# V loads on a second queue, shorter load cycles and a shorter lead of the scores in a two-problem attention kernel

## The chip, the cores and the metric

The kernel runs on one core of a Trainium2 chip. A core has a matrix engine (TensorE, PE in the profile; its weight loads are the row PEld), VectorE (DVE), ScalarE (ACT), GpSimd (POOL) and SyncE (SP), which here only issues transfers. Each engine takes its instructions in the order of the program; between engines there are semaphores. Transfers between the main memory and the core's SBUF go over 16 DMA engines; a transfer is issued by an instruction on some engine's queue.

The metric is the device time of one execution in microseconds (us). The time before is the median of three runs, 1215.2 us (1215.15 to 1217.5). The profiled execution took 1209.51 us, with a span of 1207.8 us from its first to its last instruction.

## The reference

Two independent problems, A and B, of the same shape: 16 batches, 16 heads, 144 queries, 512 keys, a head size of 256, a model width of 448. Everything is bf16.

```python
q = (x @ wq).reshape(B, Sq, H, Dh).transpose(0, 2, 1, 3)
scores = jnp.einsum("bhqd,bhkd->bhqk", q, k_cache) * (Dh ** -0.5)
p = softmax(scores, axis=-1)
o = jnp.einsum("bhqk,bhkd->bhqd", p, v_cache)
y = o.transpose(0, 2, 1, 3).reshape(B, Sq, H * Dh) @ wo
```

The output is A's y beside B's y, (16, 144, 896).

## The kernel before, in words

**Units.** A unit U is one head of one batch: 256 units of A, then 256 of B, 512 in all (`NT`). Four units make a group G, whose V (1 MB) is one transfer; eight make a super-group SG, whose K (2 MB) is one transposing transfer. There are 64 super-groups (`NSG`).

**One unit.** Its 144 queries are split into 112 (part "a") and a remainder of 32 (part "b"). On PE, a unit has `Q` (8 matmuls, the projection; line 340), `SA` (2 matmuls, scores of part a; line 476), `TA` (4 transposes of the normalised probabilities; line 530), `PV` (8 matmuls; line 563) and a share of `OP`, the output projection (line 601), which is cut into pieces and fed in by a credit. The remainders of a super-group's eight units are packed by fours on the 128 partitions, and their scores `SB` (16 matmuls; line 380) come once for each super-group. Between scores and transposes, DVE takes the row maximum (line 488; 393 for the remainder), ACT the exponential with its sum (499; 403), DVE the reciprocal (509; 413), and GpSimd multiplies by it (517, `nm`; 421, `nmb`).

**The remainder's transpose.** It has two ways. Either PE transposes it (`t_tb`, line 443: 8 matmuls for each super-group, evacuated by DVE, line 453), or a transposing transfer SBUF to SBUF does it (`t_ptb_dma`, line 431, on SP's queue, which waits for `nmb`). The set `TB_SG` names the super-groups that go over PE: the first 8, and 28 to 37 around the step from A to B; 18 in all. Either way GpSimd then copies the result (`cptb`, line 463, twice for each super-group) to where `PV` reads it.

**Order.** A planner writes each engine's program slot by slot: slot i holds `PV(i)`, `TA(i + 2)`, and the scores of a unit further ahead. `LAGS` says how many units the scores of super-group n are ahead of its PV: 7, 5, 6, 7 and so on to 14 for n = 10 and later (`sb_slot[n] = 8n - lag`). `Q` is 8 units ahead of the scores.

**Transfers.** All are issued on SP's queue, in the order of a plan that is sorted by slot (`dma_plan`): x (lines 297, 298), wq (276, 278), wo (286), K (307), V (318), the remainder's transpose (431), stores (630). K has two buffers (`NK`), V five (`NV`), x two. From super-group 8 on the plan has a cycle of 16 units (t = 8n, n even): transpose of remainder n at t-4, K of n+2 at t-3, transpose of n+1 and K of n+3 at t+2, then three V at t+5 and one at t+8. So a K is issued 5 or 8 units before its SB. The wq of B are planned for slots 228.9 to 235, the wo of B for 277 and 293.

Of the kernel before, what the change touches and what calls it, by code (L numbers as in the profile page):

```python
# [12 lines left out]
PE, ACT, DVE, POOL, SP = "pe", "act", "dve", "pool", "sp"  # L13
# [109 lines left out]
def bass_concat_heads__mha_block_cached__gqa_block_cached__near_ridge_kernel(  # L123
# [15 lines left out]
    vs = (A_v_cache, B_v_cache)  # L139
# [20 lines left out]
    NPC = NWO // OPP  # L160

    LT = 2
    LAGS = (7, 5, 6, 7, 8, 9, 10, 11, 12, 13, 14)
    RAMP = 8
    TB_SG = set(range(RAMP)) | set(range(NSG // 2 - 4, NSG // 2 + 6))
    NK, NV, NXG = 2, 5, 2
    WO_AT = ((12, 18, 26, 33), (277, 277, 293, 293))
    OP_FROM = (34, 34)
    N_WARM = (12, 16)
    XB = 2  # L170
    assert Bn % XB == 0
    NQT, NPA, NPB, NPT, NST, NSTB, NOST = 12, 14, 2, 8, 4, 2, 3
    NPBT = 1
    RS = 4
    KR = 4
# [3 lines left out]
    NXGT = NP * Bn // XB  # L179
# [3 lines left out]
    with contextlib.ExitStack() as es:  # L183
        def sb(name, shape, dt):
            return es.enter_context(nc.sbuf_tensor(name, shape, dt))
# [12 lines left out]
        pb_sb = sb("pb_sb", [128, NPB, 2, SK], BF16)  # L198
        pt_sb = sb("pt_sb", [128, NPT, 4, SQ], BF16)
        pbt_sb = sb("pbt_sb", [128, NPBT, 2, 4, 128], BF16)  # L200
        ost_sb = sb("ost_sb", [128, NOST, D], BF16)
        ident = sb("ident", [128, 128], BF16)
        stat = sb("stat", [128, 3 * NST + 3 * NSTB + 2], F32)
# [108 lines left out]
        def t_load_v(G):  # L312
            pr, b, h0 = unit(4 * G)
            sl = G % NV
            src = vs[pr][b, h0:h0 + 4].rearrange("u (p c) d -> p u (c d)", p=128)

            def e(q):
                return q.dma_start(v_sb[:, sl, :, :], src).then_inc(sems["v%d" % sl], 16)
# [107 lines left out]
        def t_ptb_dma(SG):  # L426
            psl = SG % NPB
            tsl = SG % NPBT

            def e(q):  # L430
                return q.dma_start_transpose(pbt_sb[:, tsl, :, :, :].rearrange("p g c q -> p (g c) q"),
                                             pb_sb[:, psl, :, :].rearrange("p g k -> p (g k)")).then_inc(
                    sems["pb%d" % tsl], 16)
            S.add(SP, e, reads=[(("pb", psl, g), (2 * SG + g, 1)) for g in range(2)],
                  writes=[(("pbt", tsl, g), SG) for g in range(2)], dma_sem="pb%d" % tsl, name="pb%d" % SG)

        def t_tb(G):
            psl = (G // 2) % NPB
# [44 lines left out]
        def t_max(U):  # L483
# [3 lines left out]
            def e(v):  # L487
# [2 lines left out]
            S.add(DVE, e, reads=[(("sap", bank), ("s", U))], writes=[(("neg", sl), U)], banks=["sa%d" % bank],  # L490
                  name="mx%d" % U)

        def t_exp(U):
            bank = U % 2
            sl = U % NST
            psl = U % NPA

            def e(a):
                return a.activation(pa_sb[0:QA, psl, :], sa_ps[bank][0:QA, :], AF.Exp,  # L499
                                    bias=stat[0:QA, NEG + sl:NEG + sl + 1], scale=1.0,  # L500
                                    accum_out=stat[0:QA, RSUM + sl:RSUM + sl + 1])
            S.add(ACT, e, reads=[(("sap", bank), ("s", U)), (("neg", sl), U)],
                  writes=[(("pa", psl), (U, 0)), (("rsum", sl), U)], banks=["sa%d" % bank], name="ex%d" % U)

        def t_recip(U):
            sl = U % NST
# [4 lines left out]

        def t_norm(U):
            sl = U % NST
            psl = U % NPA

            def e(g):
                return g.tensor_tensor(pa_sb[0:QA, psl, :], pa_sb[0:QA, psl, :],  # L517
                                       stat[0:QA, RINV + sl:RINV + sl + 1].to_broadcast([QA, SK]), op=ALU.mult)
            S.add(POOL, e, reads=[(("pa", psl), (U, 0)), (("rinv", sl), U)], writes=[(("pa", psl), (U, 1))],
                  name="nm%d" % U)  # L520

        def t_ta(U):
            psl = U % NPA
            bank = ta_bank[U]

            def e(t):
                src = pa_sb[0:QA, psl, :].rearrange("q (c p) -> q c p", c=4)
                ins = None
                for c in range(4):
                    ins = t.transpose(pta_ps[bank][:, c * 128:c * 128 + QA], src[:, c, :], ident[0:QA, 0:QA])  # L530
# [126 lines left out]
        def plan(at, lo, dl, fn, *args):  # L657
            assert lo <= at <= dl, (fn.__name__, args, lo, at, dl)
            dma_plan.append((at, len(dma_plan), fn, args))

        def plan_x(at, XG):
            n = XB * H
            plan(at, q_slot[(XG - 1) * n - 1] + 1 if XG >= NXG else s_min, q_slot[XG * n], t_load_x, XG)

        def plan_k(at, SG):
            plan(at, sa_slot[8 * (SG - NK) + 7] + 1 if SG >= NK else s_min, sb_slot[SG], t_load_k, SG)

        def plan_v(at, G):
            lo = 4 * (G - NV) + 3 + 1 if G >= NV else s_min
            plan(max(at, lo), lo, 4 * G, t_load_v, G)  # L670

        def plan_pb(at, SG):
            if SG not in TB_SG:
                plan(at, sb_slot[SG] + 5, 8 * SG - 1, t_ptb_dma, SG)

        plan_x(s_min, 0)
        for hg in range(HG):
            plan(s_min + (0 if hg < 2 else 1), s_min, q_slot[4 * hg], t_load_wq, 0, hg)
            if hg == 1:
                plan_k(s_min, 0)  # L680
        plan_v(s_min + 2, 0)
        for n in range(1, RAMP + 2):
            at = max(sb_slot[n] - 6, sa_slot[8 * (n - NK) + 7] + 1) if n >= NK else s_min + 2
            if n == 3:
                plan_x(at, 1)
            if n == 6:
                plan_x(at, 2)
# [58 lines left out]
        while True:  # L746
# [151 lines left out]
```

## Time and profile before

| What | Before |
|---|---|
| median of 3 runs | 1215.2 us |
| profiled execution, its own time | 1209.51 us |
| its span | 1207.8 us |
| PE busy | 1167.9 us (97%) |
| VectorE, ScalarE, GpSimd busy | 743.6, 747.8, 727.0 us |
| granted PE clock, mean | 0.994 of full |
| DMA | 306.18 MB, mean 254 GB/s |
| median time from issue to landing: K (A, B), V, remainder's transpose | 12.2 and 11.5, 9.0, 4.7 us |

Busy time of PE is modelled from pipelined matmuls, so a busy PE is not one at its peak. A DMA-issuing instruction does not count as busy time of its engine. A wait line reads: who waited, at which line, for whom; then the total in us, how often, and the longest. In a table by windows, the columns are the busy us of PE, PEld, DVE, ACT and POOL with the number of instructions, then the granted clock of PE, the DMA engines' busy share (over 1 where packets overlap) and GB/s. "SPq" is SP's queue: start, and how long the issuing instruction held the queue.

### The profile page before, as it was taken

The numbers are of one execution on the slowest core, as the hardware profiler recorded it, in microseconds if no ns is written. First come the engines' busy times: TensorE is split into PE (matmuls) and PEld (weight loads), VectorE is DVE, ScalarE is ACT, GpSimd is POOL, SyncE is SP. The second block draws the span as 40 slices with busy tenths as digits, with TensorE's granted clock in tenths as the row PEclk, the third lists the DMA queues.
The fourth block names the chain that finished last, engine by engine and source line by source line (L and its number), as shares of the span: only waits on it lengthen the run. The fifth ranks groups of instructions, "written<-read, shape, count | busy, mean of one in ns | idle before, by whom it ended". The sixth has DMA issues, their size and how long they took to land.

```text
span 1207.8 us, 33200 instructions
## 1 busy us (share of the span) xinstructions
PE 1167.9 (97%) x13612; PEld 875.3 (72%) x13612; DVE 743.6 (62%) x2088; ACT 747.8 (62%) x2213; POOL 727.0 (60%) x774
## 2 busy tenths in 40 slices
PE   6898999999999999999899999999999999999989
PEld 4676777777777777777577777777777777777766
DVE  3676666666666656666466665665666566566661
ACT  2565666666666666666466666666666666566662
POOL 1676576666666566666465665666666665666661
PEclk9999999999999999999899999999999999999999
DMA  9999999999999999999999899999999999999981
GB/s 243 284 262 294 283 277 188 253 264 269 268 283 206 264 253 293 259 263 245 288 249 255 249 265 277 261 279 251 268 236 248 253 292 274 231 251 252 249 207 56
DMA packets 679577, 306.18 MB, mean 254 GB/s; under 512 B 597504, under 2 KB 610304, under 8 KB 679424
## 3 DMA queue, kind: packets, MB, share of 16 engines
q1 hardware_dynamic: 679424, 304.05, 104.1%
q8 instruction: 107, 1.75, 0.6%
q14 instruction: 46, 0.38, 0.1%
HBM read 148.90 MB, written 4.13 MB: 127 GB/s over the span
## 4 chain that ended last, share of the span: by engine, by line
PE 81%; DMA 11%; POOL 3%; DVE 3%; SPq 1%; issue 1%; ACT 0%; DVEq 0%
PE ot_ps L563 18%; PE qp_ps L340 17%; PE sa_ps L476 17%; PE op_ps L601 16%; PE sa_ps L530 7%; DMA kt_sb<-in_B_k_cache_dram 6%; PE sb_ps L380 5%; DMA kt_sb<-in_A_k_cache_dram 5%; POOL pa_sb L517 2%; DVE stat L488 1%; SPq L307 1%; POOL pb_sb L421 1%; PE qp_ps L601 1%; PE sb_ps L443 0%; DVE qt_sb L353 0%
## 5 line engine op out<-in xcount | busy, mean ns | idle before, releaser
L517 POOL TENSOR_TENSOR pa_sb<-pa_sb,stat 112x512 bf16<-112x512 bf16 x512 | 531.4, 1039 | 453.0 <-DVE stat L509 427.4
L499 ACT ACTIVATE pa_sb<-sa_ps,stat 112x512 bf16<-112x512 f32 x512 | 352.1, 688 | 400.5 <-DVE stat L488 398.2
L488 DVE TENSOR_REDUCE stat<-sa_ps 112x1 f32<-112x512 f32 x512 | 353.8, 691 | 329.6 <-PE sa_ps L476 324.8
L340 PEld LDWEIGHTS qp_ps<-xt_sb,wq_sb 128*128 128x128 bf16 x4048 | 283.4, 98 | 81.6 <-DMA wq_sb<-in_A_wq_dram 3.6
L340 PE MATMUL qp_ps<-xt_sb,wq_sb 128*128 128x144 bf16 x4048 | 336.7, 226 | 5.0 <-DMA wq_sb<-in_A_wq_dram 4.7
L563 PE MATMUL ot_ps<-pt_sb,v_sb 128*128 128x144 bf16 x4096 | 341.5, 226 | 0.0
L476 PE MATMUL sa_ps<-kt_sb,qt_sb 128*112 128x512 bf16 x1024 | 312.6, 387 | 6.7 <-DVE pt_sb L540 5.2
L601 PE MATMUL op_ps<-wo_sb,ring 128*128 128x448 bf16 x1120 | 275.3, 353 | 0.0
L563 PEld LDWEIGHTS ot_ps<-pt_sb,v_sb 128*128 128x128 bf16 x4096 | 268.9, 98 | 0.4
L530 PEld LDWEIGHTS sa_ps<-ident,pa_sb 112*128 112x128 bf16 x2048 | 143.8, 97 | 119.0 <-ACT pa_sb L499 38.0
L540 DVE COPY pt_sb<-sa_ps 128x448 bf16<-128x448 bf16 x512 | 191.0, 373 | 19.8 <-PE sa_ps L530 19.8
L578 ACT ACTIVATE ring<-ot_ps 128x288 bf16<-128x288 f32 (+8 forms) x512 | 190.6, 372 | 19.2 <-PE ot_ps L563 19.2
L530 PE MATMUL sa_ps<-ident,pa_sb 112*128 112x112 bf16 x2048 | 185.9, 212 | 5.7 <-ACT pa_sb L499 5.7
L353 DVE TENSOR_SCALAR qt_sb<-qp_ps 128x288 bf16<-128x288 f32 x252 | 115.1, 457 | 93.4 <-PE qp_ps L340 91.6
L421 POOL TENSOR_TENSOR pb_sb<-pb_sb,stat 128x512 bf16<-128x512 bf16 x128 | 133.0, 1039 | 0.0
L476 PEld LDWEIGHTS sa_ps<-kt_sb,qt_sb 128*112 128x112 bf16 x1024 | 96.4, 130 | 46.3 <-issue 27.6
L357 ACT ACTIVATE qt_sb<-qp_ps 128x288 bf16<-128x288 f32 x254 | 105.3, 415 | 32.0 <-PE qp_ps L340 30.6
L601 PEld LDWEIGHTS op_ps<-wo_sb,ring 128*128 128x128 bf16 x1120 | 96.1, 98 | 31.9 <-issue 0.2
L499 ACT ACTIVATION_READ_ACCUMULATOR pa_sb<-sa_ps,stat 112x1 f32 x512 | 99.1, 193 | 0.0
L403 ACT ACTIVATE pb_sb<-sb_ps,stat 128x512 bf16<-128x512 f32 x128 | 88.5, 691 | 0.8
L393 DVE TENSOR_REDUCE stat<-sb_ps 128x1 f32<-128x512 f32 x128 | 87.2, 681 | 0.0
L463 POOL COPY pt_sb<-pbt_sb 128x512 bf16<-128x512 bf16 x128 | 78.0, 610 | 10.9 <-PE ot_ps L563 10.9
(33 smaller groups left out, 345.1 us busy)
## 6 DMA issues: line engine op xcount, KB each, us to landing
v_sb<-in_A_v_cache_dram SPq DMA_DIRECT2D x64, 1024.0 KB, 9.0
v_sb<-in_B_v_cache_dram SPq DMA_DIRECT2D x64, 1024.0 KB, 9.0
out_dram<-ost_sb SPq DMA_DIRECT2D x36, 112.0 KB, 9.5
wo_sb<-in_A_wo_dram SPq DMA_DIRECT2D x8, 448.0 KB, 9.3
wo_sb<-in_B_wo_dram SPq DMA_DIRECT2D x8, 448.0 KB, 5.3
wq_sb<-in_A_wq_dram SPq DMA_DIRECT2D x4, 768.0 KB, 6.0
wq_sb<-in_B_wq_dram SPq DMA_DIRECT2D x4, 768.0 KB, 10.5
pbt_sb<-pb_sb SPq DMA_TRANSPOSE x46, 4.7
```

The source lines that it names most:

```text
L340: ins = t.matmul(acc[:, dc * SQ:(dc + 1) * SQ], lhsT=wq_sb[:, kc, c0:c0 + 128], rhs=xt_sb[:, xsl, kc, xo:xo + SQ], start=(kc == 0 and dc = ...
L353: return v.tensor_scalar(qt_sb[:, sl, :, :], src, 1.0 / 16.0, None, op0=ALU.mult)
L421: return g.tensor_tensor(pb_sb[:, psl, G % 2, :], pb_sb[:, psl, G % 2, :], stat[:, RINVB + sl:RINVB + sl + 1].to_broadcast([128, SK]), op= ...
L476: ins = t.matmul(sa_ps[bank][0:QA, :].rearrange("q (k r) -> q k r", k=KR), lhsT=qt_sb[:, U % NQT, dc, 0:QA], rhs=kt_of(U, dc), start=(dc = ...
L488: return v.tensor_reduce(stat[0:QA, NEG + sl:NEG + sl + 1], sa_ps[bank][0:QA, :], axis=AX.X, op=ALU.max, negate=True)
L499: return a.activation(pa_sb[0:QA, psl, :], sa_ps[bank][0:QA, :], AF.Exp, bias=stat[0:QA, NEG + sl:NEG + sl + 1], scale=1.0, accum_out=stat ...
L517: return g.tensor_tensor(pa_sb[0:QA, psl, :], pa_sb[0:QA, psl, :], stat[0:QA, RINV + sl:RINV + sl + 1].to_broadcast([QA, SK]), op=ALU.mult)
L530: ins = t.transpose(pta_ps[bank][:, c * 128:c * 128 + QA], src[:, c, :], ident[0:QA, 0:QA])
L540: return v.tensor_copy(pt_sb[:, sl, :, 0:QA], pta_ps[bank][:, 0:512].rearrange("p (c q) -> p c q", c=4)[:, :, 0:QA])
L563: ins = t.matmul(ot_ps[ob][:, dc * SQ:(dc + 1) * SQ], lhsT=v_sb[:, vsl, j, c * DH + dc * 128:c * DH + (dc + 1) * 128], rhs=pt_sb[:, sl, c, ...
L578: ins = a.activation(ring[:, 2 * h:2 * h + 2, c0:c0 + n1], src[:, :, 0:n1], AF.Copy)
L601: ins = t.matmul(acc[0:m, 0:D], lhsT=ring[:, c, col0:col0 + m], rhs=wo_sb[:, c, :], start=(c == first), stop=(c == last))
```

## The change

- Every V but V0 is issued on GpSimd's queue. V0 stays on SP's, with a semaphore of its own.
- The plan's cycle of 16 units goes. Each K is issued as soon as the scores that read its buffer before are through, 8 units before its SB. Each V from group 5 on is issued one unit after its buffer's last PV (slot 4(G-5)+5); V1 to V4 at slots -2, 1, 4 and 7.
- `LAGS` becomes 5, 5, 6, 7, 8, 9, 10: the lead ends at 10 units and is reached with super-group 6 (unit 48).
- `TB_SG` is the first 6 super-groups only; the other 58 remainders go over the transposing transfer, planned 5 units before their PV.
- x, wq of B and wo are planned for other slots. The buffers are fewer: q 12 to 9, probabilities 14 to 11, output staging 3 to 2.
- A way to send parts "a" over the transfer too (`ADMA`) is in the text but empty, and so without effect.

```diff
     LT = 2
-    LAGS = (7, 5, 6, 7, 8, 9, 10, 11, 12, 13, 14)
-    RAMP = 8
-    TB_SG = set(range(RAMP)) | set(range(NSG // 2 - 4, NSG // 2 + 6))
+    LAGS = (5, 5, 6, 7, 8, 9, 10)
+    RAMP = 6
+    TB_SG = set(range(RAMP))
+    ADMA = ()
+    NPX = 2 + len(ADMA)
     NK, NV, NXG = 2, 5, 2
-    WO_AT = ((12, 18, 26, 33), (277, 277, 293, 293))
+    WO_AT = ((12, 17, 20, 28), (277, 281, 285, 289))
...
-    NQT, NPA, NPB, NPT, NST, NSTB, NOST = 12, 14, 2, 8, 4, 2, 3
+    NQT, NPA, NPB, NPT, NST, NSTB, NOST = 9, 11, 2, 8, 4, 2, 2
...
+        sem_names.append("vs")
...
-                return q.dma_start(v_sb[:, sl, :, :], src).then_inc(sems["v%d" % sl], 16)
-            S.add(SP, e, writes=[(("v", sl), G)], dma_sem="v%d" % sl, name="v%d" % G)
+                return q.dma_start(v_sb[:, sl, :, :], src).then_inc(sems["vs" if G == 0 else "v%d" % sl], 16)
+            S.add(SP if G == 0 else POOL, e, writes=[(("v", sl), G)], dma_sem="vs" if G == 0 else "v%d" % sl, name="v%d" % G)
...
         def plan_k(at, SG):
-            plan(at, sa_slot[8 * (SG - NK) + 7] + 1 if SG >= NK else s_min, sb_slot[SG], t_load_k, SG)
+            lo = sa_slot[8 * (SG - NK) + 7] + 1 if SG >= NK else s_min
+            plan(max(at, lo), lo, sb_slot[SG], t_load_k, SG)
...
-        def plan_pb(at, SG):
+        def plan_pb(SG):
             if SG not in TB_SG:
-                plan(at, sb_slot[SG] + 5, 8 * SG - 1, t_ptb_dma, SG)
+                plan(sb_slot[SG] + 5, sb_slot[SG] + 5, 8 * SG - 2, t_ptb_dma, SG)
...
-        plan_v(s_min + 2, 0)
-        for n in range(1, RAMP + 2):
-            at = max(sb_slot[n] - 6, sa_slot[8 * (n - NK) + 7] + 1) if n >= NK else s_min + 2
...
-            plan_k(at, n)
-            plan_v(at + 1, 2 * n - 1)
-            plan_v(at + 1, 2 * n)
+        plan_v(s_min, 0)
+        plan_k(s_min, 1)
+        for G in range(1, NV):
+            plan_v(sb_slot[0] + 3 * G, G)
+        for XG in range(1, NXGT):
+            t = XB * H * XG
+            plan_x(t - (30 if XG < 2 else 33.5), XG)
+        for SG in range(NSG):
+            plan_pb(SG)
+            if SG >= NK:
+                plan_k(sa_slot[8 * (SG - NK) + 7] + 1, SG)
+        for G in range(NV, NG):
+            plan_v(4 * (G - NV) + 5, G)
...
-        for n in range(RAMP, NSG, 2):
-            t = 8 * n
...
-            plan_pb(t - 4, n)
-            if n + 2 < NSG:
-                plan_k(t - 3, n + 2)
-            plan_pb(t + 2, n + 1)
-            if n + 2 < NSG:
-                plan_k(t + 2, n + 3)
-            for j, at in enumerate((5, 5, 5, 8)):
-                if 2 * n + 3 + j < NG:
-                    plan_v(t + at, 2 * n + 3 + j)
         for hg in range(HG):
             lo = q_slot[NU - H + 4 * hg + 3] + 1
-            plan((4.9, 4.9, 8, 11)[hg] + NU - 32, lo, q_slot[NU + 4 * hg], t_load_wq, 1, hg)
+            plan((226, 231, 234, 239)[hg], lo, q_slot[NU + 4 * hg], t_load_wq, 1, hg)
...
-            while stores and stores[0][1] <= i and (i % 16 in (9, 10, 11) or i >= NT - 4):
+            while stores and stores[0][1] <= i and (i % 8 in (7, 0, 1) or i >= NT - 4):
```

More of the change, by code (lines that the diff above doesn't have):

```diff
@@ L197, in bass_concat_heads__mha_block_cached__gqa_block_cached__near_ridge_kernel @@
         pa_sb = sb("pa_sb", [128, NPA, SK], BF16)
-        pb_sb = sb("pb_sb", [128, NPB, 2, SK], BF16)
+        pb_sb = sb("pb_sb", [128, NPB, NPX, SK], BF16)
         pt_sb = sb("pt_sb", [128, NPT, 4, SQ], BF16)
-        pbt_sb = sb("pbt_sb", [128, NPBT, 2, 4, 128], BF16)
+        pbt_sb = sb("pbt_sb", [128, NPBT, NPX, 4, 128], BF16)
         ost_sb = sb("ost_sb", [128, NOST, D], BF16)
@@ L433, in e, with by_dma, t_copy_pta @@
                     sems["pb%d" % tsl], 16)
-            S.add(SP, e, reads=[(("pb", psl, g), (2 * SG + g, 1)) for g in range(2)],
-                  writes=[(("pbt", tsl, g), SG) for g in range(2)], dma_sem="pb%d" % tsl, name="pb%d" % SG)
+            S.add(SP, e, reads=[(("pb", psl, g), (2 * SG + g, 1)) for g in range(2)] +
+                  [(("pb", psl, 2 + k), ("a", 8 * SG + j, 1)) for k, j in enumerate(ADMA)],
+                  writes=[(("pbt", tsl, g), SG) for g in range(NPX)], dma_sem="pb%d" % tsl, name="pb%d" % SG)
+        def by_dma(U):
+            return U % 8 in ADMA and U // 8 not in TB_SG
+        def t_copy_pta(U):
+            SG = U // 8
+            tsl = SG % NPBT
+            k = 2 + ADMA.index(U % 8)
+            def e(g):
+                return g.tensor_copy(pt_sb[:, U % NPT, :, 0:QA], pbt_sb[:, tsl, k, :, 0:QA])
+            S.add(POOL, e, reads=[(("pbt", tsl, k), SG)], writes=[(("pta", U % NPT), U)], name="cpta%d" % U)
         def t_tb(G):
@@ L491, in t_max, with p_of @@
                   name="mx%d" % U)
+        def p_of(U):
+            if by_dma(U):
+                psl, k = (U // 8) % NPB, 2 + ADMA.index(U % 8)
+                return pb_sb[0:QA, psl, k, :], ("pb", psl, k), ("a", U)
+            psl = pa_slot[U]
+            return pa_sb[0:QA, psl, :], ("pa", psl), (U,)
         def t_exp(U):
@@ L495, in t_exp @@
             sl = U % NST
-            psl = U % NPA
+            dst, key, ver = p_of(U)
             def e(a):
-                return a.activation(pa_sb[0:QA, psl, :], sa_ps[bank][0:QA, :], AF.Exp,
+                src = sa_ps[bank][0:QA, :]
+                return a.activation(dst, src, AF.Exp,
                                     bias=stat[0:QA, NEG + sl:NEG + sl + 1], scale=1.0,
@@ L502, in t_exp @@
             S.add(ACT, e, reads=[(("sap", bank), ("s", U)), (("neg", sl), U)],
-                  writes=[(("pa", psl), (U, 0)), (("rsum", sl), U)], banks=["sa%d" % bank], name="ex%d" % U)
+                  writes=[(key, ver + (0,)), (("rsum", sl), U)], banks=["sa%d" % bank], name="ex%d" % U)
         def t_recip(U):
@@ L513, in t_norm @@
             sl = U % NST
-            psl = U % NPA
+            dst, key, ver = p_of(U)
             def e(g):
[L517 to L520, printed above, removed]
+                return g.tensor_tensor(dst, dst, stat[0:QA, RINV + sl:RINV + sl + 1].to_broadcast([QA, SK]),
+                                       op=ALU.mult)
+            S.add(POOL, e, reads=[(key, ver + (0,)), (("rinv", sl), U)], writes=[(key, ver + (1,))], name="nm%d" % U)
         def t_ta(U):
-            psl = U % NPA
+            psl = pa_slot[U]
             bank = ta_bank[U]
@@ L639, in bass_concat_heads__mha_block_cached__gqa_block_cached__near_ridge_kernel @@
         ta_bank = {}
+        pa_slot = {}
+        for u in range(NT):
+            if not by_dma(u):
+                pa_slot[u] = len(pa_slot) % NPA
         lag = [LAGS[min(n, len(LAGS) - 1)] for n in range(NSG)]
@@ L670, in plan_v @@
             plan(max(at, lo), lo, 4 * G, t_load_v, G)
-        def plan_pb(at, SG):
+        def plan_pb(SG):
             if SG not in TB_SG:
-                plan(at, sb_slot[SG] + 5, 8 * SG - 1, t_ptb_dma, SG)
+                plan(sb_slot[SG] + 5, sb_slot[SG] + 5, 8 * SG - 2, t_ptb_dma, SG)
         plan_x(s_min, 0)
         for hg in range(HG):
-            plan(s_min + (0 if hg < 2 else 1), s_min, q_slot[4 * hg], t_load_wq, 0, hg)
+            plan(s_min, s_min, q_slot[4 * hg], t_load_wq, 0, hg)
             if hg == 1:
                 plan_k(s_min, 0)
-        plan_v(s_min + 2, 0)
-        for n in range(1, RAMP + 2):
-            at = max(sb_slot[n] - 6, sa_slot[8 * (n - NK) + 7] + 1) if n >= NK else s_min + 2
[L684 to L687, printed above, removed]
-            plan_k(at, n)
-            plan_v(at + 1, 2 * n - 1)
-            plan_v(at + 1, 2 * n)
+        plan_v(s_min, 0)
[11 more added lines that the diff above has]
+            plan_v(4 * (G - NV) + 5, G)
         for pr in range(NP):
@@ L693, in bass_concat_heads__mha_block_cached__gqa_block_cached__near_ridge_kernel @@
                 plan(WO_AT[pr][wg // 2], s_min, pr * NU + OP_FROM[pr] + wg, t_load_wo, pr, wg)
-        for n in range(RAMP, NSG, 2):
-            t = 8 * n
-            XG = (t + 32) // (XB * H)
-            if (t + 32) % (XB * H) == 0 and XG < NXGT:
-                plan_x(t - 4, XG)
-            plan_pb(t - 4, n)
-            if n + 2 < NSG:
-                plan_k(t - 3, n + 2)
-            plan_pb(t + 2, n + 1)
-            if n + 2 < NSG:
-                plan_k(t + 2, n + 3)
-            for j, at in enumerate((5, 5, 5, 8)):
-                if 2 * n + 3 + j < NG:
-                    plan_v(t + at, 2 * n + 3 + j)
         for hg in range(HG):
             lo = q_slot[NU - H + 4 * hg + 3] + 1
-            plan((4.9, 4.9, 8, 11)[hg] + NU - 32, lo, q_slot[NU + 4 * hg], t_load_wq, 1, hg)
+            plan((226, 231, 234, 239)[hg], lo, q_slot[NU + 4 * hg], t_load_wq, 1, hg)
         dma_plan.sort(key=lambda t: t[:2])
@@ L788, in bass_concat_heads__mha_block_cached__gqa_block_cached__near_ridge_kernel @@
                 t_copy_ptb((i + 3) // 4)
+            for k, j in enumerate(ADMA):
+                u = i + j - (1 if j > 2 else 0)
+                if (i - (1 if j > 2 else 0)) % 8 == 0 and 0 <= u < NT and by_dma(u):
+                    t_copy_pta(u)
             for u in sa_at.get(i - 1, ()):
@@ L792, in bass_concat_heads__mha_block_cached__gqa_block_cached__near_ridge_kernel @@
             u = i + LT
-            if 0 <= u < NT:
+            if 0 <= u < NT and not by_dma(u):
                 ta_bank[u] = 1 - last_sa % 2 if sas else u % 2
```

## The prediction

> **What bounds the kernel now.** I read the busy times first, then a table by windows (in the middle of problem A, and after each long stall), then the waits, then the chain and SP's queue around the longest wait.
>
> ```profile
> PE 1167.9 (97%) x13612; PEld 875.3 (72%) x13612; DVE 743.6 (62%) x2088; ACT 747.8 (62%) x2213; POOL 727.0 (60%) x774
> ```
> ```profile
> 200.00:236.00 36.00, 36.00 (x425) 27.37 (x425) 22.67 (x64) 23.12 (x65) 22.78 (x24) 1.00 1.00 254
> 600.00:607.00 7.00, 7.00 (x60) 4.30 (x53) 3.05 (x9) 1.99 (x6) 1.17 (x2) 0.69 1.32 278
> 108.00:112.00 4.00, 3.86 (x33) 2.29 (x34) 1.34 (x3) 0.78 (x2) 0.00 (x0) 0.68 1.06 389
> ```
>
> In the middle PE is busy without a break, and two super-groups take 36 us (the chain's SB starts lie 18.0 apart: 217.07, 235.03, 253.13). This stretch is bound by PE, and GpSimd has 18.0 - 11.4 = 6.6 us free in each super-group. So only the places where PE waits, and PE work that goes, can give time.
>
> ```profile
> POOL pa_sb L517 <- DVE stat L413: 25.4, 1, 25.4
> ...
> PE sb_ps L380 <- DMA kt_sb<-in_B_k_cache_dram: 8.7, 4, 5.8
> PE sa_ps L530 <- ACT pa_sb L499: 5.7, 9, 0.7
> PE sa_ps L476 <- DVE pt_sb L540: 5.2, 9, 1.3
> PE sb_ps L380 <- DMA kt_sb<-in_A_k_cache_dram: 5.2, 3, 3.7
> ```
>
> PE's longest waits are for K, 13.9 us: at 88 and 108 us in the ramp, and at 600, 711 and 749 us around the step to B. The granted clock then is 0.69 over the 7 us behind the 5.8 us wait (2.2 us lost) and 0.68 over 4 us around the end of the 3.7 us one (1.3 us lost).
>
> ```profile
> 565.03 6.26 SPq L318 DMA_DIRECT2D v_sb<-in_A_v_cache_dram  x4
> 571.34 2.81 SPq L276 DMA_DIRECT2D wq_sb<-in_B_wq_dram  x1
> 574.19 2.32 SPq L278 DMA_DIRECT2D wq_sb<-in_B_wq_dram  x1
> 576.55 0.63 SPq L630 DMA_DIRECT2D out_dram<-ost_sb  x1
> 577.23 0.54 SPq L276 DMA_DIRECT2D wq_sb<-in_B_wq_dram  x1
> 577.81 2.87 SPq L278 DMA_DIRECT2D wq_sb<-in_B_wq_dram  x1
> 580.73 24.39 SPq L307 DMA_TRANSPOSE kt_sb<-in_B_k_cache_dram  x2
> ```
> ```profile
> 580.73 19.00 DMA kt_sb<-in_B_k_cache_dram
> 599.73 0.14 issue
> 599.86 1.90 PE sb_ps L380 x14
> ```
> ```profile
> L307 SPq DMA_TRANSPOSE kt_sb<-in_B_k_cache_dram x32: 7577/8647/16566, 580.7 to 1143.2; - x32
> L318 SPq DMA_DIRECT2D v_sb<-in_B_v_cache_dram x64: 367/507/1897, 605.8 to 1178.6; - x64
> ```
>
> One queue carries all: a K holds SP 7.6 to 16.6 us, and a K behind four V and the wq lands 19 us after its issue, against 9.6 at best. By the landings that the trace records, a K right behind another transfer takes 7.25 us (V0 landed at 30.21, K1 at 37.46) to 9, a V 2.6, a wo 1.2, an x about 1.5.
>
> **The change part by part.**
>
> *Transposes leave PE.* 12 super-groups x 8 = 96 matmuls of line 443 go; back to back they start 55 ns apart in the trace, so 5.3 us of PE. The 16 in the ramp lie beside K-bound stretches; the 80 around the step count: -4.4 (ends -5.3 and 0, if transfers set that stretch). 24 DVE evacuations go too, on an engine 62% busy: nothing. In their place come 12 more transfers by line 431. Their median landing is 4.7 us, and from issue (slot 8n-5) to the copy (8n-1) there are 4 slots x 2.25 = 9 us; what covers them is this slack.
>
> *V leaves SP's queue.* SP sheds 127 issues of 0.51 us; no wait ended on them alone: nothing. GpSimd gains 127 issues. The trace has no transfer issued there. Below is SP's 0.37 to 0.51 us for a V; above, the 7.6 us that a K holds SP. Nearest are 0.51 and GpSimd's own `nm` of 1.04; as GpSimd also computes, I take 1.5. The waits for PE in front of a V are met by then (its buffer's PV is a slot old), so nothing queues for that. Two V in a super-group make 11.4 + 3.0 = 14.4 of 18.0 us, hidden under PE; the cover is gone at 6.6 / 2 = 3.3 us for a V. Queued behind each V are `nm` and `cptb`; `nm` has about 7 slots until its TA.
>
> *The start.* There GpSimd is on the path: its first `nm` ends a wait of 25.4 us, and nm, nmb, nm, nm, nmb run without a gap from 26.7 to 31.9 while PE waits for each in turn. V1 and V2 now lie in this chain: 2 x 1.5 = +3 (ends +0.8 by the 0.4 us rows, +6.6 at 3.3 us).
>
> *The ramp.* The lags of super-groups 1 to 6 are as before. The waits of today (5.2 + 1.3 of slow clock = 6.5) stem from wo and V in front of K4 and K5 on one queue. Now V no longer stands in that queue, but V1 to V5 are issued earlier, and the same 16 DMA engines carry them: until K2 is in, the ledger is K1 40 us (37.46 plus V1), x 1.5, V2, V3, V5, V4 10.4, K2 7.25 = 59; SB2 is due at SB1 (about 42, with the start's loss) + 15.6 (56.24 - 40.61 now) = 58. With a V6 in front too, 62. So a new wait of about 2.5 us at SB2, with up to 1 us of slow clock: +3.5. Afterwards seven slots of 15.6 us stand against K + 2 V = 7.25 + 5.2, plus at most four wo 4.8: about even. Net -3 (ends -6.5 and +6).
>
> *The end of the ramp.* A lead of 10 instead of 14 moves four units' Q and scores from early to late, work that PE does anyway: 0. Half a K less must be in by any slot; this helps K only.
>
> *K as soon as its buffer is free.* From 5 or 8 slots to 8 for all: 18 us, against 7.25 + 5.2 + about 2 of latency = 14.5. K waits of the steady part (0.35 us at 1108) go.
>
> *The step to B.* Waits 8.7 + 2.2 of slow clock = 10.9. Over slots 222 to 246, three super-groups (54 us), the transfers are 3 x (7.25 + 5.2 + 1.2 for the remainder and stores) + 4 wq of 0.9 MB at 2.5 + x 1.5 = 52.5: it just fits, where now the gaps between issues on one queue are lost too. One wq stands in front of K32 and K33: 2.5 us may be left. -8.4 (ends -10.9 and 0).
>
> *Buffers and stores.* q 9, probabilities 11, output 2: each is rewritten at least one slot after its last reader on PE; the stores lie 14 units apart. 0; at the tail, where the last chunks come close, +-2.
>
> Sum: -4.4 + 3 - 3 - 8.4 = -12.8 on the profiled 1209.5, so 1196.7. That execution lies 5.7 below the median of the runs shown (1215.2), where I forecast **1202.4**. The forecast's own range, by all lower ends, is 1191 (-5.3 + 0.8 - 6.5 - 10.9 - 2 = -23.9), and to 1213 if one of the two stalls stays.
>
> **Rivals.**
>
> *V and K share the engines to no gain* (ends on the other side). One queue's trace shows a pure K stretch at 290 GB/s and a pure V one at about 385, so little is idle while something is queued; V, now issued first, takes its time out of K. Place: SB2 to SB6 in the ramp, and K32, K33, where the wait stays. It decides if each K takes its 9 us plus two V in full: K2 then lands 2 to 5 us later, and wo and V before K5, K6 (9 + 5.2 + 4.8 = 19 > 15.6) add 3 more: ramp +6, step 0. Sum -4.4 + 3 + 6 + 0 = +4.6: **1219.8**. For it: 19 us for K32. Against: the 1 us gaps at each change of kind on the one queue. [...]
>
> *GpSimd becomes the bound.* If a V costs it over 3.3 us, every super-group grows by twice the rest: at 4 us, 57 x 2 x 0.7 = +80, less 12.8: **1282**; it would run away at the 7.6 us end. For it: nothing but the missing row. Against: V's 0.51 us on SP.
>
> *The remainder's transpose comes late.* Line 431 on SP waits behind a K that V makes longer, its copy on GpSimd then holds `PV` at line 563. It decides past 9 us from slot 8n-5 to landing; median now 4.7, longest 11.3. At half a us in each of 57 super-groups +28, less 12.8: **1230**.
>
> *The step stays.* wq in front of K32 costs as now, the rest goes as forecast: -4.4: **1210.8**.
>
> **How the numbers follow.** Chances: forecast 0.53, shared engines 0.14, late transposes 0.11, GpSimd bound 0.11, step stays 0.11. 0.2% (2.4 us) is about what a measurement of this kernel can tell from no change. Faster: nearly all of the forecast (0.51) and 0.08 of "step stays" = 0.59; same 0.07, from the upper end of these and the lower of the first rival; slower 0.34. The range goes from 1191 to 1240: it leaves out the GpSimd bound and a little on either side.
>
> **What would show it.** Right: no transposes of line 443 after about 120 us; waits at SB for K under 6 us in all, none of 5 us near 600 us; the middle still 18.0 us for a super-group, PE unbroken; V's issuing rows on GpSimd 1 to 2 us; K landings shorter than 19 us at the most. Wrong: `PV` waiting for GpSimd's copy or `TA` for `nm` in the middle (GpSimd or the late transpose); SB waiting in every super-group (shared engines); V rows over 3.3 us.

## The result, and the profile after

The changed kernel takes 1331.9 us in the median of four runs (1308.5 to 1357.9), against 1216.3 us for the kernel before on the same chip. Two of the four executions (1349.9 and 1357.9 us) took over 3% longer than the fastest, for a reason that no trace here shows, and are left out of the comparison: the other two, 1308.5 and 1313.9 us, stand at 1.078 times the kernel before (95% interval 1.0736 to 1.0825). The forecast was 1202.4 us, its range ended at 1240. The profiled execution took 1308.52 us, with a span of 1306.8.

The busy times of the changed kernel (engine, us, share of the span, instructions):

```profile
PE 1181.0 (90%) x13516; PEld 881.6 (67%) x13516; DVE 733.6 (56%) x2064; ACT 744.5 (57%) x2213; POOL 820.6 (63%) x901
```

The span grew by 99.0 us. PE is busy 13.1 us longer, although 96 matmuls (5.3 us) are gone: the same work took some 18 us more, with its clock granted at 0.958 on the mean, against 0.994 before. PE stands idle 125.8 us, against 39.9 before: +85.9. (GpSimd's count of instructions grew from 774 to 901, by the 127 issues of V: here they do count as busy time, other than those on SP.) The list of waits says for whom (who, line, whom; total us, times, longest):

```profile
PE sb_ps L383 <- DMA kt_sb<-in_A_k_cache_dram: 57.7, 10, 17.4
...
PE sb_ps L383 <- DMA kt_sb<-in_B_k_cache_dram: 34.0, 7, 14.6
...
POOL pt_sb L479 <- DMA pbt_sb<-pb_sb: 28.6, 8, 7.2
...
PE ot_ps L586 <- POOL pt_sb L479: 13.8, 4, 5.9
```

The scores `SB` wait 91.7 us for K, against 13.9 before (+77.8); `PV` waits 13.8 us for GpSimd's copy of the remainder, which itself waited for the transposing transfer, against 0 before. Two smaller waits, around `SA` and `TA`, fell by 5.3. Together that is +86.3, so no other wait is needed for the idle time.

The losses are stalls at a few places, not a slower rhythm. Here is the table by windows of the changed kernel (us, then busy us and instructions of PE, PEld, DVE, ACT and POOL, the granted clock, DMA share, GB/s): the middle of A is as before, PE unbroken at full clock, while in an 18 us stretch of the ramp PE does next to nothing, and in a 20 us stretch after the step it is busy for less than half, at low clocks both times.

```profile
40.00:58.00 18.00, 0.57 (x9) 0.21 (x10) 0.00 (x0) 0.79 (x4) 0.49 (x1) 0.56 1.24 109
440.00:480.00 40.00, 40.00 (x473) 30.46 (x471) 25.74 (x73) 26.58 (x85) 29.40 (x34) 1.00 1.14 252
...
756.00:776.00 20.00, 9.62 (x88) 6.41 (x87) 4.66 (x12) 5.39 (x20) 4.58 (x5) 0.66 1.16 218
```

The DMA share is 1.24 in the first of these rows, and only 109 GB/s move: the engines are occupied, and little comes through. SP's queue there, and the chain of work that ended last (start, us, what):

```profile
21.04 22.10 SPq L310 DMA_TRANSPOSE kt_sb<-in_A_k_cache_dram  x1
43.18 3.62 SPq L300 DMA_TRANSPOSE xt_sb<-in_A_x_dram  x1
46.84 2.65 SPq L301 DMA_TRANSPOSE xt_sb<-in_A_x_dram  x1
49.53 14.10 SPq L310 DMA_TRANSPOSE kt_sb<-in_A_k_cache_dram  x1
```
```profile
21.04 36.61 DMA kt_sb<-in_A_k_cache_dram
57.65 0.04 issue
57.70 1.90 PE sb_ps L383 x9
```

K1 needed 36.6 us from issue to landing, where the worst K of the kernel before needed 19.0. Two V had been issued behind it on GpSimd's queue, at 30.02 and 36.00 us (landed at 40.65 and 57.60). The issues of V themselves cost GpSimd little; the lines by source, K's line 310 first (durations of the issuing instruction in ns, min/median/max), then V's 321:

```profile
L310 SPq DMA_TRANSPOSE kt_sb<-in_A_k_cache_dram x32: 7952/12346/22097, 5.9 to 624.3; - x32
...
DMA to landing us min/median/max: 10.8/18.0/36.6
```
```profile
L321 POOL DMA_DIRECT2D v_sb<-in_B_v_cache_dram x64: 789/789/798, 655.0 to 1266.2; - x64
...
DMA to landing us min/median/max: 5.6/8.4/21.6
```

A K now lands 18.0 us after its issue in the median (before 12.2 in A and 11.5 in B), which is just the 18 us that a super-group lasts. V lands in 8.4 us. So V is served and K pays.

### The profile page after: what moved, and what is told of

Its sections match the earlier page's. It is cut to its first block, busy times and chain, and to the rows that moved or that the text cites. A ratio compares the mean times of both kernels' runs of the same rounds, so it can differ in the third digit from the quotient of the medians.

```text
span 1306.8 us, 33018 instructions
## 1 busy us (share of the span) xinstructions
PE 1181.0 (90%) x13516; PEld 881.6 (67%) x13516; DVE 733.6 (56%) x2064; ACT 744.5 (57%) x2213; POOL 820.6 (63%) x901
## 4 chain that ended last, share of the span: by engine, by line
PE 64%; DMA 29%; SPq 3%; POOL 2%; DVE 1%; issue 1%; DVEq 0%
PE ot_ps L586 14%; PE sa_ps L492 14%; PE qp_ps L343 14%; PE op_ps L624 13%; DMA kt_sb<-in_B_k_cache_dram 12%; DMA kt_sb<-in_A_k_cache_dram 12%; PE sa_ps L553 5%; PE sb_ps L383 4%; DMA pbt_sb<-pb_sb 4%; POOL pa_sb L541 1%; SPq L310 1%; SPq L300 1%; SPq L301 0%; PE qp_ps L624 0%; DVE stat L504 0%
## 5 line engine op out<-in xcount | busy, mean ns | idle before, releaser
L586 PE MATMUL ot_ps<-pt_sb,v_sb 128*128 128x144 bf16 x4096 | 345.3, 227 | 14.1 <-POOL pt_sb L479 13.8
L343 PE MATMUL qp_ps<-xt_sb,wq_sb 128*128 128x144 bf16 x4048 | 340.7, 228 | 5.2 <-DMA wq_sb<-in_A_wq_dram 4.3
L343 PEld LDWEIGHTS qp_ps<-xt_sb,wq_sb 128*128 128x128 bf16 x4048 | 287.9, 99 | 81.0 <-issue 4.6
L492 PE MATMUL sa_ps<-kt_sb,qt_sb 128*112 128x512 bf16 x1024 | 318.8, 394 | 5.3 <-DVE pt_sb L563 4.3
L586 PEld LDWEIGHTS ot_ps<-pt_sb,v_sb 128*128 128x128 bf16 x4096 | 271.9, 98 | 15.5 <-POOL pt_sb L479 15.1
L553 PEld LDWEIGHTS sa_ps<-ident,pa_sb 112*128 112x128 bf16 x2048 | 146.6, 98 | 114.9 <-ACT pa_sb L523 28.5
L383 PE MATMUL sb_ps<-kt_sb,qt_sb 128*32 128x512 bf16 x1024 | 72.6, 407 | 91.8 <-DMA kt_sb<-in_A_k_cache_dram 57.7
L383 PEld LDWEIGHTS sb_ps<-kt_sb,qt_sb 128*32 128x32 bf16 x1024 | 22.5, 99 | 116.4 <-DMA kt_sb<-in_B_k_cache_dram 35.3
```

Of the source, the lines that this page charges most:

```text
L343: ins = t.matmul(acc[:, dc * SQ:(dc + 1) * SQ], lhsT=wq_sb[:, kc, c0:c0 + 128], rhs=xt_sb[:, xsl, kc, xo:xo + SQ], start=(kc == 0 and dc = ...
L383: ins = t.matmul(sb_ps[jj // 4][32 * j:32 * j + 32, :].rearrange("q (k r) -> q k r", k=KR), lhsT=qt_sb[:, U % NQT, dc, QA:SQ], rhs=kt_of(U ...
L492: ins = t.matmul(sa_ps[bank][0:QA, :].rearrange("q (k r) -> q k r", k=KR), lhsT=qt_sb[:, U % NQT, dc, 0:QA], rhs=kt_of(U, dc), start=(dc = ...
L586: ins = t.matmul(ot_ps[ob][:, dc * SQ:(dc + 1) * SQ], lhsT=v_sb[:, vsl, j, c * DH + dc * 128:c * DH + (dc + 1) * 128], rhs=pt_sb[:, sl, c, ...
```

## Is it the queue, or the rest of the change?

**The change, with V back on SP (e1).** Everything of the change stays, its plan of slots too.

```diff
-            S.add(SP if G == 0 else POOL, e, writes=[(("v", sl), G)], ...
+            S.add(SP, e, writes=[(("v", sl), G)], ...
```

> The changed kernel with every V back on SP's queue, at the slots of the new plan; all else of the change stays. Theory 'two queues' (K and V in flight from two queues move fewer bytes: 242 GB/s while both are in flight in the changed kernel, 50 to 80 in its long waits, against 264 on one queue): the K waits go, 1195 to 1225 us. Theory 'plan' (V issued earlier and the lead of 10 units take K's time on any queue): 1280 us or more, SB still waiting over 100 us for K.

Measured: 1228.1 us (1225.4 to 1230.8), 1.0113 times before (1.0093 to 1.0133). So some 83 us of the loss hang on the queue (1311.2, the mean of 1308.5 and 1313.9, less 1228.1), and the rest of the change is not free either. SP's queue in that kernel at the same place, and its waits:

```profile
20.95 14.41 SPq L310 DMA_TRANSPOSE kt_sb<-in_A_k_cache_dram  x1
35.41 1.13 SPq L321 DMA_DIRECT2D v_sb<-in_A_v_cache_dram  x2
```
```profile
POOL pt_sb L479 <- DMA pbt_sb<-pb_sb: 71.0, 33, 8.4
...
PE ot_ps L586 <- POOL pt_sb L479: 27.0, 14, 6.4
PE sb_ps L383 <- DMA kt_sb<-in_A_k_cache_dram: 11.6, 5, 5.1
```

K1 holds SP 14.4 us instead of 22.1, and lands at 39.0 instead of 57.7; its wait is gone, and K's waits are back to 13.9 us in all. What is left is the late transpose of the remainder, 27.0 us of `PV` waits: on one queue with all the rest this small transfer lands 7.2 us after its issue in the median, 4.7 before.

**V on ScalarE's queue (e2).** The same line, with `ACT` in place of `POOL`.

> [...] 'Two queues' in general: 1280 to 1360 us, K landing about 18 us after issue. If only GpSimd's way of issuing is at fault: 1195 to 1225 us with K landing in about 12. 'Plan': 1280 or more.

Measured: 1252.1 and 1272.3 us in two runs, no interval. In the profile, of the longer one, K's waits are 55.3 us in all, the longest 19.8. A second queue costs much here whoever issues, so it isn't GpSimd alone; but the loss, 38 to 58 us over the kernel before (1214.1 here), is some half of that with GpSimd's queue.

**The kernel before, with V1 and later on GpSimd at the old slots (e3).**

```diff
-            S.add(SP, e, writes=[(("v", sl), G)], dma_sem="v%d" % sl, name="v%d" % G)
+            S.add(SP if G == 0 else POOL, e, writes=[(("v", sl), G)], dma_sem="vs" if G == 0 else "v%d" % sl, ...
```

> The kernel before with V1 to V127 on GpSimd's queue, at the slots of the old plan; nothing else of the change. 'Two queues': 1260 to 1340 us, SB waiting over 60 us for K. 'Plan': about 1216 us.

Measured: 1223.5 us, 1.0075 (1.0055 to 1.0096). The same second queue costs 9 us under the old plan and 83 under the new one. The waits of this kernel:

```profile
PE sb_ps L381 <- DMA kt_sb<-in_B_k_cache_dram: 11.5, 5, 5.1
...
PE sb_ps L444 <- POOL pb_sb L422: 10.5, 8, 1.7
...
PE qp_ps L341 <- DMA wq_sb<-in_A_wq_dram: 9.3, 2, 6.9
...
PE sb_ps L381 <- DMA kt_sb<-in_A_k_cache_dram: 1.1, 3, 0.8
```

The ramp's waits for K are nearly gone (1.1 us), as the prediction had it. K32 still comes 5.1 us late, and V issued early now delays wq, by 6.9 us. The 10.5 us at line 444, against 1.2 before, are another matter: in the ramp PE's transposes of the remainder wait for `nmb`, five times for 1.7 us, each right after GpSimd has issued two V. In all K's waits are 12.6 us, fewer than the 13.9 before. So what this kernel loses is the issuing and wq, and not a slow K; the 9 and the 83 us are not the same loss.

**The kernel before, with the remainder transposed by transfers around the step (e4).** `TB_SG` becomes the first 8 super-groups only.

```diff
-    TB_SG = set(range(RAMP)) | set(range(NSG // 2 - 4, NSG // 2 + 6))
+    TB_SG = set(range(RAMP))
```

> The kernel before with the remainders of super-groups 28 to 37 over the transposing transfer as well, nothing else. By the prediction's first term (80 transposes of 55 ns) 4.4 us faster, 1210 to 1213 us; if the transfers set the stretch around the step to B, 0 to 6 us slower, 1216 to 1222.

Measured: 1216.9 us, 1.0022 (1.0008 to 1.0036) over ten runs. The 80 transposes that left PE gave nothing. The 5.8 us that `SB` waited for K32 became 5.8 us in which `PV` waits for the copy:

```profile
POOL pt_sb L463 <- DMA pbt_sb<-pb_sb: 10.1, 2, 6.8
...
PE ot_ps L563 <- POOL pt_sb L463: 8.2, 2, 5.8
```

## What two queues do to each other

**Transfers alone (t1 to t4).** Nothing is computed here. 24 K, and in the first three 48 V beside them: on one queue, with V on GpSimd's, with V on ScalarE's; t4 has K only. The core of it is this, with `q` the issuing engine (waits and semaphores left out, and the target of K shortened):

```python
def load_k(q, n):
    src = A_k_cache.rearrange("b h k d -> (b h k) d")[n * 8 * SK:(n + 1) * 8 * SK, :]
    q.dma_start_transpose(kt[:, n % 2]..., src.rearrange("(r k) d -> r (k d)", k=KR))
def load_v(q, n):
    b, h0 = divmod(4 * n, 16)
    q.dma_start(v[:, n % 5, :, :], A_v_cache[b, h0:h0 + 4].rearrange("u (p c) d -> p u (c d)", p=128))
```

> Transfers alone, no computing: 24 K (2 MB, transposing, two buffers) and 48 V (1 MB, five buffers) of problem A, all on SP's queue in the order K, V, V; a load waits only for the load that filled its buffer before, and at the end 18 stores write zeros. From the landings on one queue (K 7.25 to 9 us behind another transfer, V 2.6): 24 x (7.25 to 9 + 5.2) = 299 to 341 us, and about 20 for start and stores; 100.7 MB at 300 to 335 GB/s.

> Transfers alone as in the one-queue kernel, with the V on GpSimd's queue, kept in step with K (V of a super-group waits for the K of two before, and K for the V of that time), so that both are in flight together nearly always. 'Two queues' (fewer bytes when both are in flight): 242 GB/s as in the changed kernel gives 416 us, and more if the slow stretches of 50 to 80 GB/s set in. If mixing costs nothing: as the one-queue kernel or shorter, 300 to 340.

> The same with the V on ScalarE's queue. 'Two queues' whatever the issuer: as with GpSimd's, over 400 us. If GpSimd's way of issuing is at fault: 300 to 340.

> Transfers alone: the 24 K on SP's queue, no V. 24 x 7.25 to 9 = 174 to 216 us and about 20 for start and stores. It gives the share of K in the other three.

Measured (two executions each): 354.5 us on one queue, 358.4 with GpSimd's, 327.7 with ScalarE's, 209.5 for K alone. So the simple form of the theory, that two queues move fewer bytes, falls: issued in step, V beside K costs 1% on GpSimd's queue, and saves 8% on ScalarE's. A K and its two V take 13.7 to 14.9 us (the times over 24), less than the 18 us of a super-group. The mean rate is not what is lost.

What differs is who is served while both are under way. The DMA view of t2 over 4 us in which both are (q0 is GpSimd's queue, all V; q1 is SP's, all K; packets, MB, share):

```profile
DMA packets 767, 1.61 MB, mean 401 GB/s; under 512 B 399, under 2 KB 399, under 8 KB 767
...
q0 software_dynamic: 384, 1.51, 96.4%
q1 hardware_dynamic: 383, 0.10, 11.0%
```

The packets are equal in number, 384 (16 of them of 4 bytes, the rest V's) and 383, and unequal in size: V goes in packets of 4096 bytes, K in packets of 256. With 96 packets per us K has nearly stopped (t4 moves 1076 per us on the mean of 10 us, and up to 1135). In the changed kernel the same is seen at 31 to 34 us (K alone), at 36 to 37 (in step), and then at 43 to 50, which is another matter:

```profile
DMA packets 3373, 0.86 MB, mean 288 GB/s; under 512 B 3373, under 2 KB 3373, under 8 KB 3373
...
DMA packets 162, 0.35 MB, mean 349 GB/s; under 512 B 82, under 2 KB 82, under 8 KB 162
...
q0 software_dynamic: 80, 0.33, 81.5%
q1 hardware_dynamic: 82, 0.02, 9.3%
...
DMA packets 1229, 0.48 MB, mean 68 GB/s; under 512 B 1186, under 2 KB 1186, under 8 KB 1229
...
q1 hardware_dynamic: 1183, 0.30, 112.7%
q0 software_dynamic: 46, 0.18, 12.4%
```

From 43 to 50 us K is still slow (169 packets per us; 78 to 166 in all of these microseconds but one, which has 505), but V is slow now too: 43 packets of 4096 bytes (and 3 of 4 bytes), 6.1 per us. At 163 ns for one, the mean of the packet records from 36 to 37 us, I estimate that as the full time of one DMA engine out of 16 (6.1 x 0.163 = 1.0); from 43 to 50 us the median of their records is 166 ns, the mean 322. From 43.7 to 45.8 us these packets start 0.17 to 0.18 us apart, one after another, and K's packets of 43 to 46 us, divided by 16, are 7.5 per us beside V's 6.0. Altogether 68 GB/s, while PE stands. This is the stretch that costs. If all 16 engines moved K independently, one engine's V could not hold the other fifteen; so I asked whether K goes at the pace of its slowest engine.

**V on one engine (t5).** 8 K on SP, and beside them 40 loads on ScalarE's queue, each of one head's V (a quarter of a V above), with 127 of its 128 rows (`[0:127]` in `load_v`). When K is through, these loads move 12.5 packets of 2 KB per us, 26 GB/s, each packet taking 84 ns (6.6% of 16 engines' time over 126 packets in 10 us): by my estimate the full time of one engine (12.5 x 0.084 = 1.05).

> Transfers alone: 8 K on SP's queue, and beside them on ScalarE's queue a stream of 40 loads of 127 rows of 2 KB, which are expected to run on few DMA engines or one. Theory 'slowest engine' (a K goes forward on all 16 engines at the pace of the slowest): K falls from 1135 packets in a us to 150 to 200 as long as the stream runs, spread evenly over its time. Rival (each engine does its share of K by itself): K runs at about 1060 packets in a us for some 7 us, and only the last sixteenth of it comes slowly.

Measured: 482.1 us in one execution; a K took 54 to 61 us from issue to landing, against 9.9 to 11.0 in t4. The DMA view over 10 us with both (q1 is K, q10 the loads), and then of t4 over 10 us:

```profile
DMA packets 1822, 0.66 MB, mean 66 GB/s; under 512 B 1716, under 2 KB 1716, under 8 KB 1822
...
q1 hardware_dynamic: 1715, 0.44, 121.7%
q10 hardware_dynamic: 107, 0.22, 5.6%
```
```profile
DMA packets 10759, 2.75 MB, mean 275 GB/s; under 512 B 10759, under 2 KB 10759, under 8 KB 10759
```

K's 1715 packets over 16 engines are 107 for each, and the loads' packets are 107 as well. These are the counts that one engine alternating between the two would give, with the fifteen that have nothing but K no faster than that one; the packet records don't name the engine, so that is my reading of them. The rival, in which each engine does its share of K by itself, had 1060 packets per us for some 7 us; the records count 132 to 189 in every microsecond from 180 to 215. It falls: in t5 the transposing load went at the pace that its slowest engine would set. An estimate from the durations fits. A packet of K takes 18 ns in t4 (121.4% of 16 engines' time over 10759 packets in 10 us), one of the loads in t5 84: if they alternate, one K packet per 102 ns, 157 per us over 16 engines, where 172 are counted. With V's 163 ns it is one per 181 ns, 88 per us, near t2's 96, and near the 76 to 105 that the packet records of the changed kernel count in ten of the twenty microseconds from 35 to 55.

So, as I read it, the price of V beside K depends on how V's packets fall. At t2's 96 packets per us a V of 256 packets is through in about 3 us, an estimate, and little is lost in all (358.4 against 354.5 us). Where V's packets come one after another, 6.1 per us from 43 to 50 us, K moves 169 packets per us, against 1124 alone from 31 to 34 us, for as long as V lasts. In the changed kernel V's packets from 34 to 39 us, 249 of the 256 that one V has, go in the first way; those behind them, of the V issued at 36 us, go in the second until about 51 us. That is read from the counts and the starts; what brought them there isn't shown, as the packet records don't name the engine.

## Is it where V is issued?

**Both V of a super-group in the gap between two K (e5).** GpSimd's queue is kept; from V6 on the two V are planned together, 6 slots before the super-group that needs them, where the K before has mostly landed.

```diff
-            plan_v(4 * (G - NV) + 5, G)
+            plan_v(8 * (G // 2) - 6 if G // 2 >= 3 else 4 * (G - NV) + 5, G)
```

> The changed kernel with both V of a super-group issued together on GpSimd's queue, from group 6 on at slot 8m-6, in the gap after one K and before the next, where the change has one at 8m-7 and one at 8m-3, the second in the middle of the next K. Theory 'overlap' (a V in flight from a second queue goes in front of a K packet by packet, and its last packets hold the K on all engines): the K waits from 280 us on fall by half or more, 1250 to 1285 us. If the loss is only that of the first 160 us, or of the plan's early K: no change, 1300 to 1315.

Measured: 1222.5 us, 1.0054 (1.0026 to 1.0083): some 89 us of the 95 come back, more than I expected. GpSimd still issues all V but V0, so its way of issuing alone doesn't make the 89 us. By the issues and landings in the trace, K and V are both under way for 368 us, against 975 in the changed kernel. The waits of e5:

```profile
POOL pt_sb L479 <- DMA pbt_sb<-pb_sb: 32.2, 18, 6.3
...
PE sb_ps L383 <- DMA kt_sb<-in_A_k_cache_dram: 19.5, 3, 16.6
...
PE ot_ps L586 <- POOL pt_sb L479: 14.6, 7, 5.0
...
PE sb_ps L383 <- DMA kt_sb<-in_B_k_cache_dram: 2.3, 2, 1.5
```

One wait of 16.6 us is left, at the second super-group, where V1 and V2 are still issued behind K1 as in the changed kernel.

**Only the ramp's V on SP (e6),** V0 to V14, the rest on GpSimd at the change's slots.

```diff
-            S.add(SP if G == 0 else POOL, e, writes=[(("v", sl), G)], ...
+            S.add(SP if G < 15 else POOL, e, writes=[(("v", sl), G)], ...
```

> The changed kernel with V0 to V14 on SP's queue (used to about unit 60), the rest on GpSimd's as in the change. 'Overlap': the three waits of the ramp (17.4, 12.7 and 15.8 us at SB and the slow clock behind them, about 60 us in all) fall to those of the one-queue version (5.2 and 4.0), the later ones stay: 1255 to 1275 us. If the ramp's plan itself is at fault: 1300 or more.

Measured: 1282.1 us (1274.9 and 1289.2), 1.056 (1.048 to 1.064); worse than expected. The 17 us wait of the ramp goes, but others come where V next falls on K: 14.5 us at 167, 13.7 at 746, 12.4 at 1180. The slow stretches aren't a matter of the ramp alone; these three have V from GpSimd's queue beside the K that is late, and their places move with small shifts of the plan.

**The old plan with V0 to V4 on SP and the rest on GpSimd (e7).**

```diff
-            S.add(SP, e, writes=[(("v", sl), G)], dma_sem="v%d" % sl, name="v%d" % G)
+            S.add(SP if G < 5 else POOL, e, writes=[(("v", sl), G)], ...
```

> The kernel before with V5 to V127 on GpSimd's queue, V0 to V4 on SP's (with all but V0 on GpSimd's it took 1223.5 us, with a wait of 6.9 us for wq at 8 us and five of 1.7 us for nmb in the ramp). 'Overlap': the old plan issues its V after its two K, so K and V seldom overlap, and without the early V it is as before or a little faster, 1208 to 1218. If V on GpSimd's queue costs in itself: 1223 or more.

Measured: 1229.6 us (1218.4 to 1238.7 over ten runs), 1.0114 (1.008 to 1.0148). A miss, with a wide spread: it lies where the rival of this expectation had it, V on GpSimd's queue costing in itself. Of the waits, those for `nmb` are 8.7 us, as in e3 (1.2 before), and those for K 22.6 (13.9 before). The trace shows what fails around 941 us: four V were issued between 913.8 and 920.6, and an x issued at 916.4 on SP landed 20.0 us later; the K behind it held SP 16.8 us and landed 18.9 us after its issue, 4.3 us late. So x suffers as K does, and so does a remainder's transpose, issued at 923.0 and landed 14.1 us later. Why single executions differ by 20 us isn't shown.

**Ramp and gap together (e8),** and **the step's transposes on TensorE again (e9).** To e5, e8 adds that V1 to V5 go on SP, each behind the K before it; e9 adds the old set around the step.

```diff
-            S.add(SP if G == 0 else POOL, e, ...
+            S.add(SP if G < 6 else POOL, e, ...
...
-            plan_v(sb_slot[0] + 3 * G, G)
+            plan_v(sb_slot[0] + 3 * G if G < 3 else sa_slot[7] + 2, G)
...
-    TB_SG = set(range(RAMP))
+    TB_SG = set(range(RAMP)) | set(range(28, 38))
```

(The last two lines are e9's alone; V5 moves to `sa_slot[15] + 2` in both.)

> The kernel with both V of a super-group issued together on GpSimd in the gap between two K, and now also V1 to V5 on SP, each behind the K before it: V1 and V2 behind K1 as they stand, V3 and V4 one slot behind K2, V5 one slot behind K3. The kernel before this one (1222.5 us) still waited 16.6 us for K1 at its second super-group's scores, and 17.07 us of half clock followed, 8.5 us lost; V1 and V2 were issued 8.6 and 14.1 us after K1 and landed before it. Theory 'what costs is a V issued on a second queue while a K is in flight': this wait and the half clock go, some 5 us of waits of the ramp on one queue come (5.2 in the kernel before the change): 1222.5 - 25.1 + 5 = 1202, that is 1196 to 1208, below the kernel before the change. Rival 'the rest of the loss is elsewhere (the remainder's copies that PV waits for, 14.6 us, and V at large)': the ramp's wait only moves to the next K, 1215 to 1225.

> As the run before, and the remainder of the 10 super-groups around the step to B is transposed on TensorE again, as before the change. In the kernel with V apart the scores-times-V products waited 5.0, 2.7 and 4.3 us for GpSimd's copy at 596 to 736 us, behind remainder transposes that landed 9 to 13 us after their issue, and two stretches of 6.8 us of half clock followed. Theory 'the remainder's transpose comes late where wq, wo, x and V are in flight': these 12.0 us and some 6.8 us of slow clock go, 80 transposes of 55 ns = 4.4 us come: 14 us under the run before, about 1188, if nothing else is late there; by the trial of the same 10 super-groups in the kernel before the change, where K was the next to be late, only 0 to 6 us. Rival 'that trial holds here too, PE waits for something in any case': within 3 us of the run before.

Measured: e8 1214.1 us (1208.9 to 1219.8, twelve runs), 1.0005 (0.9985 to 1.0025); e9 1213.3 us, 1.0000 (0.9986 to 1.0015). The wait of 16.6 us is gone, yet only 8 of the 20 us that I expected came. The waits of e8:

```profile
PE ot_ps L587 <- POOL pt_sb L480: 14.9, 6, 5.2
...
PE sb_ps L384 <- DMA kt_sb<-in_A_k_cache_dram: 7.8, 2, 6.7
```

K4, issued at 71.9 us, met V6 and V7 (77.4 and 78.3, now the first on GpSimd's queue) and landed after 23.5 us, 6.7 late. In e9, as in e4, one wait takes the place of another: `PV` waits 7.4 instead of 14.9 us, and `SB` waits 9.8 us in one piece, at 603 us, for K32: four wq ahead of it delayed its start, the two V of the next gap (issued at 593.9 and 594.7) then fell on it, and it landed after 29.1 us. Neither beats the kernel before; I found no version that does.

## Why the prediction was wrong, point by point

**The ramp (-3, ends -6.5 and +6): the step that failed.** Its ledger added the transfers up to K2, 59 us, at a fixed price for each (7.25 us for a K, 2.6 for a V), as if the 16 engines worked off one list. K1 was entered at 40 us, V1 included; it landed at 57.7 us, and PE waited 17.4 us for it. V issued later on the other queue was served packet for packet with K (384 against 383 in t2), and from 43 to 50 us both nearly stopped (6.1 packets of V and 169 of K per us). K3 and K5 came 12.7 and 15.7 us late, each with V under way beside it: 45.8 us of waits in the ramp, where a gain of 3 was forecast, more than half of the 77.8 that K's waits grew by. The same fixed prices stood in the other terms, so the rest was missed by the same step: K60 near the end, issued at 1177.4 us with three V beside it, landed after 33.5 us, 14.6 late, and the tail I had put at 0. The direction of the forecast was wrong with it.

**K as soon as its buffer is free (18 us against 14.5).** The sum K + 2 V was about right as a rate (t1: 354.5 / 24 = 14.8 us), but a K took 18.0 us in the median and up to 36.6, and V is in flight beside K most of the time (975 of 1306.8 us). The middle held, at 18.0 us for a super-group; 17 of the 64 K came too late for their scores.

**V leaves SP's queue (0).** The cost on GpSimd was right and smaller than taken: 0.79 us against 1.5. The rival in which GpSimd becomes the bound falls (63% busy). What I priced was the issuing alone, and here it was not the issue that cost. Under the old plan it was: in e3 and e7 `nmb` behind two V cost PE 1.7 us at a time.

**Transposes leave PE (-4.4).** Failed, by e4 and e9: 0. The stretch around the step is set by transfers, which was the lower end I had given and not taken. The cover of 9 us did not hold where wq, wo and V are in flight: `PV` waits 27.0 us in e1.

**The step to B (-8.4).** It didn't come: at 759.6 us `SB` waits 10.4, and between 585 and 653 `PV` waits 3.2, 1.9 and 5.9 for the copy.

**The start (+3)** can't be told apart: the lag is another there, and the PE reaches its wait for K1 at 40.3 us.

**The rivals.** "V and K share the engines to no gain" had the place, the ramp, and the direction, with 0.14; its price of +17 over the forecast let each K pay for the V beside it at full rate, where K's rate beside a V fell to a twelfth (96 packets per us in t2, up to 1135 alone in t4) and, from 43 to 50 us, V's fell too (6.1 per us, 96 in t2). The sign that I gave for it, `SB` waiting in every super-group, did not come: 17 of 64 waited. "The remainder's transpose comes late" is a true part: 13.8 us of waits here and 27.0 in e1, against its price of 28, but in 4 and 14 places and not in each of 57 super-groups.

As far as the total of the transfers goes, the first of these holds on GpSimd's queue (358.4 us, against 354.5 on one) and not on ScalarE's (327.7). What it would have taken to see the result is that one queue's packet here is 16 times as large as the other's (4096 against 256 bytes).

## What to carry to other kernels

Before moving a load to a second queue, look at the packets: a transposing load in packets of 256 bytes came to a near standstill here beside one in packets of 4096 (96 packets per us in t2, up to 1135 alone in t4), so the total may hold (358.4 against 354.5 us) while the load that PE waits for is late. If two queues are wanted, issue the large transfers in the gaps of the small ones, or in one queue behind them; e5 against the change, with one line of the plan, was worth 89 us. A sum of durations against a period is a test of rate alone, and says nothing of who is served first.

## What of the hardware I had not expected

- With work on both, two queues got equal numbers of packets in t2: over 4 us, 383 of K's, of 256 bytes, and 384 of GpSimd's, 368 of them of 4096 bytes. From ScalarE's queue V goes in packets of 2048 bytes (t3, 100 to 150 us: 8.21 MB in 4125 packets, 114 of them small). If the two queues alternate there too, the 390 GB/s or so that t3 moves in its mixed stretches are about 170 packets of each per us; that is an estimate. In t2 K keeps 96, alone up to 1135 (t4).
- A transposing load went at the pace that its slowest engine would set: 1715 packets in 10 us, 107 for each of 16 engines, with 107 packets of another load beside them (t5).
- K slows behind instruction fetches too. In the kernel before there are 107 of them, each one packet of 16 KB, 1.09 us long on the mean. Its DMA view at 379 to 389 us (40 slices of 0.25 us), with one fetch at 383.3:

```profile
GB/s 152 85 119 185 215 253 198 191 285 290 291 291 288 292 290 291 290 343 216 37 0 7 9 10 94 287 289 293 289 288 293 294 285 291 293 289 318 274 260 10
...
q8 instruction: 1, 0.02, 0.6%
```

K falls from 290 GB/s to 37 and less for 1.25 us behind it. On the mean of the 60 fetches of 16 KB that fell into a stream of K in this kernel (over 500 of K's packets in the microsecond before), K moves 10 GB/s from 0.5 to 1.75 us after the fetch's start.
